# GraphSAGE neighbour sums on one core: the source one-hots are made in their load buffers, 36 buckets in each of five

## The chip, the core and the metric

The kernel runs on one core of a Trainium2 chip. The metric is the device time of one execution in microseconds, start to end. The core's engines each work through their own queue in order: TensorE (PE, with its weight loads shown apart as PEld), VectorE (DVE), ScalarE (ACT), GpSimd (POOL) and SyncE (SP, which here only starts transfers). Transfers between device memory and the on-chip memory are carried by DMA engines. An engine that needs the result of another waits on semaphores.

## What is computed

There are 12,500 nodes with 64 features each, and 800,000 edges with a random source and a random destination. Each node gets the sum of the features of its neighbours, scaled by `deg_inv`, multiplied by one 64 x 64 matrix, and its own features multiplied by another:

```python
N, deg, D = 12500, 64, 64
E = N * deg
src = randint(0, N, E); dst = randint(0, N, E)
nsum = segment_sum(x[src], dst, N)          # one row for each destination
h_neigh = nsum * deg_inv[:, None]
return x @ w_self + h_neigh @ w_neigh
```

## The kernel before, in words

The kernel sorts the edges and then turns the gather and the scatter into matrix products with one-hot matrices. Nodes are cut into 98 source blocks of 128 nodes (`NB`) and 77 destination blocks of 164 nodes, each of two halves of 82 (`HN`). A pair of a destination block and a source block is a **bucket**: there are 77 x 98 = 7546 of them (`NBID`), and each holds at most 64 edges to either half in 128 slots; the few that do not fit are **leftovers**. The first 800 us sort the edges on DVE (sorting steps and merges, lines 260, 316, 328, 362) and write, for each bucket, the source number of each slot to a table `sl` in device memory, and the destination number of each slot to `dlT` on the chip.

The part that the change touches is `nodes`. It handles the buckets in groups of 8, called **tiles** here, 943 of them. For one tile:

- PE makes 8 products `ct` (line 945): the one-hots of the sources of a bucket (`ohs`, as weights) times the features of the source block (`xh`). This picks the source rows.
- ACT (line 955), or for some late tiles DVE (line 953), copies `ct` from the accumulators to `xg`.
- PE makes 16 products into `acc` (line 1025): `xg` (as weights) times the one-hots of the destinations (`ohd`). This adds the rows up by destination.

The one-hots come in chunks of 28 buckets from `one_hots`. For each chunk, SP loads the source numbers, repeated over all 128 partitions, into `slb` with four transfers (line 912, three buffers); DVE compares them with the partition number and writes `ohs` (line 914, three buffers of its own); DVE compares the destination numbers in `dlT` with a ramp and writes `ohd` (line 919, four buffers). `AHEAD` says how many buckets must have their one-hots written, in program order, beyond the tile that PE is given: 44, so that a chunk is asked for at the first tile where fewer than 52 are ready.

Nothing but the order in which the program is written sets the order of work on an engine. Into the DVE queue go, between the one-hots, pieces of the merges that still have to be done for the later parts of the sort. They are given out by `PACE`: 330 ns of merge work (by the program's own estimate) for each tile while one part is merged, 265 ns while the next is. When the first merges of a part are through, `split_rows` stores the rows, counts them, and has POOL gather them in eight transfers (line 556); the merges after that (first line 316) read what was gathered. Its last `yield` says how many tiles pass before those merges are put in the queue.

Leftovers are added by `pick` (POOL fetches their source rows into `lx`, line 976), `spread` (DVE makes their destination one-hots `ohl`, line 985) and `add` (PE, line 993). `HELD` is the number of `lx` and `ohl` buffers, five. POOL also issues the gathers of the sort and adds the finished rows to the output (line 1101).

## Time and profile before

| what | value |
|---|---|
| median of three runs | 1874.64 us (1874.48 to 1878.96) |
| time of the profiled execution | 1869.61 us |
| its span, first to last instruction | 1867.8 us |
| mean granted TensorE clock | 0.806 |
| first load of source numbers (start of `nodes`) | 802.7 us |
| start of the last one-hot of sources on DVE | 1845.3 us |
| ACT copies `xg`, line 955 | 918, 862.4 us busy |
| DVE copies `xg`, line 953 | 32, 39.0 us busy |
| DVE source one-hots, line 914 | 270, 323.6 us busy |
| DVE destination one-hots, line 919 | 270, 362.0 us busy |

Times are counted from the first instruction of the span. In a row of a wait, the engine and line that waited stand first, then what released it, then the microseconds in total, how often, and the longest. In rows of a group of instructions stand the busy time, the mean in ns of one, and the idle time before them with what ended it. In the rows of a timeline stand the start, the duration, the engine, the line and the operation, and in brackets the idle time before it and its releaser.

### The profile page before, as it was taken

How to read it: one execution, taken by the hardware profiler on the slowest of the kernel's cores; microseconds unless marked ns; L12 is line 12 of the kernel's file. 1: busy time of each engine (PE TensorE's matmuls, PEld its weight loads, DVE VectorE, ACT ScalarE, POOL GpSimd, SP SyncE). 2: the span in 40 equal slices, each digit the busy share in tenths (PEclk: the TensorE clock that was granted, in tenths of full speed). 3: DMA queues.
4: the chain of work that ended last, by engine and by line, in shares of the span. 5: the costliest groups of instructions: out<-in, count | busy, mean ns of one | idle time of the engine just before them, and what ended most of it. 6: DMA issues, size and time to landing. Idle time of an engine off the chain costs nothing.

```text
span 1867.8 us, 54105 instructions
## 1 busy us (share of the span) xinstructions
PE 974.5 (52%) x23374; PEld 844.1 (45%) x23374; DVE 1730.9 (93%) x1731; ACT 1126.5 (60%) x1592; POOL 565.5 (30%) x447
## 2 busy tenths in 40 slices
PE   0035100000000000058878989897888999889996
PEld 0014100000000000057767878776777888778885
DVE  8999999999999999989979999999986999888985
ACT  7263100113001005457989999899898999878885
POOL 2000000055512005404535445473315324431331
PEclk9997555555555555579999999999999999989998
DMA  4306200021002002168968898987897899978994
GB/s 156 71 0 161 45 0 0 37 78 51 17 5 71 11 0 81 48 205 248 283 207 261 268 269 255 288 264 221 221 307 204 286 272 269 300 190 269 278 266 128
DMA packets 176788, 307.77 MB, mean 165 GB/s; under 512 B 127885, under 2 KB 133340, under 8 KB 175772
## 3 DMA queue, kind: packets, MB, share of 16 engines
q1 hardware_dynamic: 98268, 275.58, 45.3%
q0 software_dynamic: 78272, 28.65, 9.4%
q8 instruction: 184, 3.01, 0.6%
q14 instruction: 64, 0.52, 0.1%
HBM read 277.01 MB, written 26.52 MB: 163 GB/s over the span
## 4 chain that ended last, share of the span: by engine, by line
DVE 20%; PE 15%; issue 10%; DMA 9%; ACT 7%; SPq 4%; POOL 2%; DVEq 0%; ACTq 0%; POOLq 0%
DMA slb<-sl 8%; PE ct L945 8%; DVE u L328 7%; PE acc L1025 6%; ACT xg L955 5%; SPq L912 4%; DVE ohs L914 4%; DVE ohd L919 3%; DVE u L362 2%; DVE u L316 1%; POOL out L1101 1%; PE acc L993 1%; PE po L1092 1%; POOL u L556 0%; DMA lx<-xt,ls 0%
## 5 line engine op out<-in xcount | busy, mean ns | idle before, releaser
L955 ACT ACTIVATE xg<-ct 128x1024 f16<-128x1024 f32 x918 | 862.4, 1059 | 115.1 <-PE ct L945 71.9
L945 PE MATMUL ct<-xh,ohs 128*128 128x128 f16 x7546 | 529.6, 222 | 76.9 <-DVE ohs L914 24.3
L945 PEld LDWEIGHTS <-ohs 128*128 128x128 f16 x7546 | 447.2, 99 | 116.3 <-DVE ohs L914 54.8
L328 DVE TENSOR_TENSOR u<-u 128x1512 f32<-128x1512 f32 (+57 forms) x316 | 427.0, 1362 | 12.0 <-ACT u L312 7.9
L1025 PE MATMUL acc<-ohd,xg 64*128 64x82 f16 x15092 | 401.2, 201 | 56.3 <-issue 29.4
L1025 PEld LDWEIGHTS <-xg 64*128 64x128 f16 x15092 | 326.4, 96 | 117.0 <-issue 42.5
L914 DVE TENSOR_SCALAR ohs<-slb,pidx 128x3584 f16<-128x3584 bf16 x270 | 323.6, 1198 | 48.5 <-PE ct L945 22.6
L976 POOL DMA_INDIRECT lx<-xt,ls x127 | 227.4, 1791 | 460.9 <-PE acc L993 386.0
L919 DVE TENSOR_TENSOR ohd<-iota,dlT 128x2296 f16<-128x2296 bf16 x270 | 362.0, 1341 | 0.0
L500 PE MATMUL stp<-cx,swapa 128*128 128x16 f32 (+1 forms) x12 | 3.1, 335 | 394.3 <-DVE swapa L496 394.3
L260 DVE TENSOR_TENSOR a<-b 128x1040 f32<-128x1040 f32 (+41 forms) x130 | 194.7, 1539 | 4.0 <-DVE b L260 0.5
L260 DVE TENSOR_TENSOR b<-a 128x1040 f32<-128x1040 f32 (+46 forms) x150 | 194.6, 1345 | 3.2 <-ACT a L262 0.4
L529 POOL DMA_INDIRECT u<-d,ixa x48 | 72.5, 1510 | 391.4 <-ACT junka L517 335.7
L500 PEld LDWEIGHTS stp<-cx,swapa 128*128 128x128 f32 x12 | 2.6, 272 | 394.9 <-DVE swapa L496 210.3
L312 ACT ACTIVATE u<-u 128x256 f32<-128x256 f32 (+14 forms) x60 | 32.9, 611 | 163.5 <-DVE u L316 127.6
L1101 POOL DMA_DIRECT2D out<-o x27 | 100.9, 3866 | 94.1 <-ACT o L1095 75.8
L791 PE MATMUL tr<-idb,l 128*128 128x128 bf16 x59 | 7.8, 269 | 189.0 <-ACT l L785 189.0
L262 ACT ACTIVATE b<-a 128x2 f32<-128x2 f32 (+31 forms) x41 | 15.9, 401 | 130.0 <-DVE a L260 119.7
L791 PEld LDWEIGHTS <-l 128*128 128x128 bf16 x59 | 4.4, 116 | 191.3 <-ACT l L785 190.9
L316 DVE TENSOR_TENSOR u<-u 128x2016 f32<-128x2016 f32 (+11 forms) x40 | 62.5, 1574 | 18.0 <-DMA lx<-xt,ls 16.0
L262 ACT ACTIVATE a<-b 128x1 f32<-128x1 f32 (+24 forms) x34 | 8.6, 258 | 111.0 <-DVE b L260 105.6
L953 DVE CAST xg<-ct 128x1024 f16<-128x1024 f32 x32 | 39.0, 1221 | 22.5 <-PE ct L945 19.3
(157 smaller groups left out, 825.3 us busy)
## 6 DMA issues: line engine op xcount, KB each, us to landing
slb<-sl SPq DMA_DIRECT2D x1076, 224.0 KB
xt<-xh SPq DMA_DIRECT2D x1, 3136.0 KB
out<-o POOLq DMA_DIRECT2D x25, 123.0 KB
own<-os SPq DMA_DIRECT2D x12, 256.0 KB
out<-os SPq DMA_DIRECT2D x12, 256.0 KB
rd<-dst SPq DMA_DIRECT2D x4, 521.0 KB
rs<-src SPq DMA_DIRECT2D x4, 521.0 KB
lx<-xt,ls POOLq DMA_INDIRECT x127
```

Of the source, the lines that this page charges most:

```text
L260: nc.vector.tensor_tensor(view(dst, lo + sh, [[st, g], [1, l]]), x, y, op=op)
L316: nc.vector.tensor_tensor(at(oth, to, n), x, y, op=op)
L328: nc.vector.tensor_tensor(to, at(cur, ln + lo, n), at(cur, lo + k, n), op=op)
L529: nc.gpsimd.indirect_dma_start(out=u[:, i * w:(i + 1) * w], out_offset=None, in_=src, in_offset=bass.IndirectOffsetOnAxis(ap=self.start[pa ...
L912: nc.sync.dma_start(b[j::4], bass.AP(tensor=src.tensor, offset=src.offset, ap=[[0, 32], [1, n * 128]]))
L914: nc.vector.tensor_scalar(s.rearrange("p c s -> p (c s)"), b, self.pidx[:, :1], None, op0=OP.is_equal)
L919: nc.vector.tensor_tensor(d, self.iota[:, None].to_broadcast(wide), ix, op=OP.is_equal)
L945: nc.tensor.matmul(ct[:, i * 128:(i + 1) * 128], cols[i][0], self.xh[:, (b0 + i) % NB].rearrange("p a f -> p (a f)"), start=True, stop=True)
L955: nc.scalar.activation(xg[:, :cnt * 128], ct[:, :cnt * 128], AF.Copy)
L976: nc.gpsimd.indirect_dma_start(out=x, out_offset=None, in_=self.xt, in_offset=bass.IndirectOffsetOnAxis(ap=self.left[p][1][:, c:c + 1].bit ...
L1025: nc.tensor.matmul(acc[h][:, db % OCT * HN:(db % OCT + 1) * HN], xg[r, i * 128:(i + 1) * 128], d[r], start=db % OCT == 0 and sb == 0, stop ...
L1101: nc.gpsimd.dma_start(out, o[:n, at], accum_op=OP.add)
```

## The change

Every edit is in the supply of one-hots or near it:

- The loads write straight into the buffers `ohs`, and DVE writes the source one-hots over the numbers it compares, in place (both types are 16 bits wide). There are five such buffers of 36 buckets in place of three of `slb` and three of `ohs` of 28. So there are 210 source chunks for 270, and a load of 1,179,648 bytes for 917,504.
- The destination one-hots keep 28 buckets to a chunk and get a fifth buffer. The two kinds are now asked for apart: destinations at 60 buckets ahead, sources at 76 (`AHEAD` plus `FURTHER`).
- The one-hots of leftovers are stored in two blocks of 82 for each half in place of six; the comparisons are of the same size as before.
- `pick` counts a leftover buffer as taken until six tiles after its products were issued (`BACK`), so POOL is not sent for a row while its buffer is still read.
- `split_rows` lets nine tiles pass in place of five before the next merges are queued.
- `fill(4e3)` puts some 4 us of merges into the DVE queue ahead of the first one-hots.

```diff
@@ -63,7 +63,7 @@
 BIGBITS = 0x7E000000
 BIG = float(np.array(BIGBITS, np.uint32).view(np.float32))
 SIG = 5.5
-AHEAD = 44
+AHEAD = 60
 APART = 30
...
 SIGMA = 6.0
@@ -71,7 +71,11 @@
 BEHIND = 5e3
 NEARLY = 24
 LAG = 4
+FURTHER = 16
+SCH = 36
+DCH = 28
 HELD = 5
+BACK = 6
 OCT = 6
 OCTM = 256 // OCT + 1
 assert all((b * OCTM) >> 8 == b // OCT for b in range(NDB))
@@ -558,7 +562,7 @@
                 in_offset=bass.IndirectOffsetOnAxis(ap=ix[:, j:j + 1], axis=0))
             self.pause(1)
             yield 1
-        yield 5
+        yield 9
 
     def merge_runs(self, lens, u, pong, nruns, last=False):
 
@@ -900,34 +904,43 @@
         self.left[part] = (place, s)
         yield 1
 
-    def one_hots(self, pool):
-
-
-        nc = self.nc
-        for c in range(0, NBID, 28):
-            n = min(28, NBID - c)
-            b = pool.tile([128, 28 * 128], BF, name="slb", bufs=3)[:, :n * 128]
+    def source_hots(self, pool):
+
+
+        nc = self.nc
+        for c in range(0, NBID, SCH):
+            n = min(SCH, NBID - c)
+            b = pool.tile([128, SCH * 128], BF, name="ohs", bufs=5)[:, :n * 128]
             src = self.sl[c:c + n]
             for j in range(4):
                 nc.sync.dma_start(b[j::4], bass.AP(tensor=src.tensor, offset=src.offset, ap=[[0, 32], [1, n * 128]]))
-            s = pool.tile([128, 28, 128], FH, name="ohs", bufs=3)[:, :n]
-            nc.vector.tensor_scalar(s.rearrange("p c s -> p (c s)"), b, self.pidx[:, :1], None, op0=OP.is_equal)
-            d = pool.tile([128, 14, HN, 2], FH, name="ohd", bufs=4)[:, :n // 2]
+            s = b.bitcast(FH)
+            nc.vector.tensor_scalar(s, b, self.pidx[:, :1], None, op0=OP.is_equal)
+            yield [s[:, j * 128:(j + 1) * 128] for j in range(n)]
+
+    def dest_hots(self, pool):
+
+
+        nc = self.nc
+        for c in range(0, NBID, DCH):
+            n = min(DCH, NBID - c)
+            d = pool.tile([128, DCH // 2, HN, 2], FH, name="ohd", bufs=5)[:, :n // 2]
             at = c % TURN
             wide = [128, n // 2, HN, 2]
             ix = self.dlT[:, at:at + n].rearrange("p (c t) -> p c t", t=2)[:, :, None, :].to_broadcast(wide)
             nc.vector.tensor_tensor(d, self.iota[:, None].to_broadcast(wide), ix, op=OP.is_equal)
-            yield [(s[:, j], d[:, j // 2, :, j % 2]) for j in range(n)]
+            yield [d[:, j // 2, :, j % 2] for j in range(n)]
 
     def nodes(self, pool, aps, mps):
 
 
         nc = self.nc
-        source = self.one_hots(pool)
-        ready = []
+        sources, dests = self.source_hots(pool), self.dest_hots(pool)
+        ready, spare = [], []
         pend = []
         late = []
         done = []
+        added = []
         acc = None
 
         turn = 0
@@ -937,15 +950,20 @@
             nonlocal turn
             ct = aps.tile([128, 1024], F32, name="ct", bufs=3)
             ahead = AHEAD - 8 * vector
-            while len(ready) < min(cnt + ahead, NBID - b0):
-                ready.extend(next(source))
-            cols = ready[:cnt]
+            rest = NBID - b0
+            while len(ready) < min(cnt + ahead + FURTHER, rest) or len(spare) < min(cnt + ahead, rest):
+                if len(ready) <= len(spare) + FURTHER and len(ready) < rest:
+                    ready.extend(next(sources))
+                else:
+                    spare.extend(next(dests))
+            cols = list(zip(ready[:cnt], spare[:cnt]))
             del ready[:cnt]
+            del spare[:cnt]
             for i in reversed(range(cnt)):
                 nc.tensor.matmul(ct[:, i * 128:(i + 1) * 128], cols[i][0],
                                  self.xh[:, (b0 + i) % NB].rearrange("p a f -> p (a f)"), start=True, stop=True)
             xg = pool.tile([128, 1024], FH, name="xg", bufs=6)
-            if vector and (len(ready) < min(8 + ahead, NBID - b0 - cnt) or NBID - b0 < 56):
+            if vector and (len(spare) < min(8 + ahead, NBID - b0 - cnt) or NBID - b0 < 56):
                 turn += 1
             else:
                 vector = False
@@ -966,7 +984,8 @@
                         uses.append([o, p, c, f // NB, -(-e // NB), None, None, None])
 
         def pick(b0):
-            if self.picked == len(done) or len([u for u in uses if u[5]]) >= HELD:
+            held = len([u for u in uses if u[5]]) + len([n for n in added if n > len(done) - BACK])
+            if self.picked == len(done) or held >= HELD:
                 return
             u = next((u for u in uses if not u[5]), None)
             if u and u[1] in self.left and b0 + LEAD >= u[4] * NB:
@@ -980,17 +999,19 @@
 
         def spread(u):
             o, p, c, f, e = u[:5]
-            u[7] = pool.tile([128, 2, OCT * HN], FH, name="ohl", bufs=HELD)
+            assert e - f <= 2
+            u[7] = pool.tile([128, 2, 2 * HN], FH, name="ohl", bufs=HELD)
             n = slice((f - o * OCT) * HN, (e - o * OCT) * HN)
-            nc.vector.tensor_scalar(u[7][:, :, n], self.wide.rearrange("p (h n) -> p h n", h=2)[:, :, n],
+            nc.vector.tensor_scalar(u[7][:, :, :(e - f) * HN], self.wide.rearrange("p (h n) -> p h n", h=2)[:, :, n],
                                     self.left[p][0][:, c:c + 1], -float(o * (OCT * HN + 4096)),
                                     op0=OP.subtract, op1=OP.is_equal)
 
         def add(u, stop=False):
             o, _, _, f, e = u[:5]
+            added.append(len(done))
             n = slice((f - o * OCT) * HN, (e - o * OCT) * HN)
             for h in range(2):
-                nc.tensor.matmul(acc[h][:, n], u[5], u[7][:, h, n], start=False, stop=stop)
+                nc.tensor.matmul(acc[h][:, n], u[5], u[7][:, h, :(e - f) * HN], start=False, stop=stop)
 
         def extras(b0, cnt):
             o = b0 // (OCT * NB)
@@ -1284,6 +1305,7 @@
             t += 1400 if i < 4 else 2800
             if k < KPRS[0]:
                 t = fill(t) if t > 0 else t
+        fill(4e3)
         va.close()
         first_two.close()
 
```

The first place where the order moves is the queue of SP in the steady part of `nodes`. In the rows, `DMAHW` are the semaphores of earlier transfers, `DVE_49` and `PE_49` those of the engines. Before, two chunks of loads and the start of a third:

```order
L912 DMA slb<-sl 32x3584 [waits DMAHW5_49,DVE_49]
L912 DMA slb<-sl 32x3584 [waits DMAHW6_49]
L912 DMA slb<-sl 32x3584 [waits DMAHW7_49]
L912 DMA slb<-sl 32x3584 [waits DMAHW0_49]
L912 DMA slb<-sl 32x3584 [waits DMAHW1_49,DVE_49]
```

The same place of the changed kernel:

```order
L916 DMA ohs<-sl 32x4608 [waits DMAHW5_49,DVE_49,PE_49]
L916 DMA ohs<-sl 32x4608 [waits DMAHW6_49]
L916 DMA ohs<-sl 32x4608 [waits DMAHW7_49]
L916 DMA ohs<-sl 32x4608 [waits DMAHW0_49]
L916 DMA ohs<-sl 32x4608 [waits DMAHW1_49,DVE_49,PE_49]
```

The first of the four transfers of a chunk waited for DVE alone, which had read the buffer; now it waits for PE as well, which has to be through with the one-hots that stand in it.

The second place is the queue of DVE where the gathered rows of the second part are first read (the merge of 4 x 368, line 316 before and 320 now). Before, with the waits of each instruction (`DMASW` are POOL's transfers, here the gathers):

```order
L914 TENSOR_SCALAR ohs_4924<-slb_4919,pidx_88 128x3584 [waits DMAHW3_49,DMAHW2_49,DMAHW4_49,DMAHW1_49,PE_49]
L919 TENSOR_TENSOR ohd_4926<-iota_109,dlT_1165 128x2296 [waits PE_49]
L985 TENSOR_SCALAR ohl_4970<-wide_111,lp0_2318 128x2x164
L328 TENSOR_TENSOR u_790<-u_786 128x8x102 [waits DVE_49]
L914 TENSOR_SCALAR ohs_5048<-slb_5043,pidx_88 128x3584 [waits DMAHW6_49,DMAHW5_49,DMAHW7_49,DMAHW0_49,PE_49]
L919 TENSOR_TENSOR ohd_5050<-iota_109,dlT_1165 128x2296
L316 TENSOR_TENSOR u_782<-u_778 128x4x368 [waits DMASW4_49,DMASW3_49,DMASW6_49,DMASW2_49,DMASW7_49,DMASW1_49,DMASW0_49]
```

The same place of the changed kernel (ohs is line 918 there, ohd 931, ohl 1005):

```order
L918 TENSOR_SCALAR ohs_4468<-ohs_4468,pidx_88 128x4608 [waits DMAHW6_49,DMAHW7_49,DMAHW5_49,DMAHW0_49]
L931 TENSOR_TENSOR ohd_4485<-iota_109,dlT_1165 128x2296 [waits PE_49]
L1005 TENSOR_SCALAR ohl_4529<-wide_111,lp0_2309 128x328
L332 TENSOR_TENSOR u_790<-u_786 128x8x102 [waits DVE_49]
L1005 TENSOR_SCALAR ohl_4588<-wide_111,lp0_2309 128x2x82
L918 TENSOR_SCALAR ohs_4591<-ohs_4591,pidx_88 128x4608 [waits DMAHW3_49,DMAHW4_49,DMAHW2_49,DMAHW1_49]
L931 TENSOR_TENSOR ohd_4597<-iota_109,dlT_1165 128x2296 [waits PE_49]
L332 TENSOR_TENSOR u_790<-u_786 128x8x101
L320 TENSOR_TENSOR u_782<-u_778 128x4x368 [waits DMASW5_49,DMASW3_49,DMASW6_49,DMASW2_49,DMASW1_49]
```

A source one-hot waited for its four loads and for PE, which had to leave its buffer; now it waits for the loads alone. A destination one-hot now waits for PE at nearly every chunk. Source and destination chunks no longer come in pairs.

The third place is the start of `nodes` on DVE, before (line 846 is the last work of the sort's first part there):

```order
L846 MAX top0_1472<-e_1471 128x8 x5
L914 TENSOR_SCALAR ohs_1667<-slb_1662,pidx_88 128x3584
L919 TENSOR_TENSOR ohd_1669<-iota_109,dlT_1165 128x2296
L914 TENSOR_SCALAR ohs_1676<-slb_1671,pidx_88 128x3584
L919 TENSOR_TENSOR ohd_1678<-iota_109,dlT_1165 128x2296
L316 TENSOR_TENSOR u_778<-u_782 128x1264
```

And in the changed kernel:

```order
L850 MAX top0_1472<-e_1471 128x8 x5
L320 TENSOR_TENSOR u_778<-u_782 128x1264
L332 TENSOR_TENSOR u_782<-u_778 128x219 x2
L332 TENSOR_TENSOR u_778<-u_782 128x969 x2
L918 TENSOR_SCALAR ohs_1670<-ohs_1670,pidx_88 128x4608
L931 TENSOR_TENSOR ohd_1676<-iota_109,dlT_1165 128x2296
L918 TENSOR_SCALAR ohs_1678<-ohs_1678,pidx_88 128x4608
L931 TENSOR_TENSOR ohd_1684<-iota_109,dlT_1165 128x2296
L918 TENSOR_SCALAR ohs_1686<-ohs_1686,pidx_88 128x4608
L931 TENSOR_TENSOR ohd_1692<-iota_109,dlT_1165 128x2296
L332 TENSOR_TENSOR u_782<-u_778 128x1173
```

The merge that stood behind two chunks of each kind, and the smaller ones behind it, now stand ahead of the first source one-hot, and three chunks of each kind follow.

## The prediction

> **What bounds the kernel now.** I cut the time from the first load of source numbers into stretches, and read in each what the engines do.
>
> ```profile
> span 1867.8 us, 54105 instructions
> ```
>
> ```profile
> core 0: us, PE busy (x) PEld busy (x) DVE busy (x) ACT busy (x) POOL busy (x), PEclk, DMA share, GB/s
> 802.70:860.00 57.30, 39.26 (x852) 34.47 (x853) 50.48 (x84) 36.26 (x41) 11.30 (x10) 0.81 0.78 248
> 860.00:950.00 90.00, 78.87 (x1947) 68.78 (x1944) 72.44 (x76) 80.52 (x109) 47.36 (x35) 0.94 0.86 256
> 950.00:1200.00 250.00, 221.55 (x5768) 194.68 (x5764) 247.87 (x242) 234.20 (x279) 108.68 (x43) 1.00 0.87 262
> 1200.00:1600.00 400.00, 350.17 (x8712) 305.24 (x8711) 367.57 (x478) 368.71 (x492) 167.47 (x107) 0.97 0.86 259
> 1600.00:1850.00 250.00, 224.43 (x5789) 200.68 (x5789) 218.88 (x269) 209.05 (x261) 74.89 (x49) 0.97 0.83 250
> ```
>
> Before 802.7 us nothing but the order of a few instructions is touched. In 950 to 1200 DVE has no idle time (247.87 of 250) while ACT has 15.8 and PE 28.4: here DVE sets the pace. After 1200 DVE has slack (32.4 and 31.1), and ACT and PE alternate as the bound. So I asked for the waits of 950 to 1200 (from 940, to take in a stall ahead of it), then for those of the whole run:
>
> ```profile
> PE ct L945 <- DVE ohs L914: 20.4, 24, 3.0
> ACT xg L955 <- PE ct L945: 17.4, 24, 2.4
> DVE u L316 <- DMA lx<-xt,ls: 9.3, 1, 9.3
> ```
>
> ```profile
> PE ct L945 <- DVE ohs L914: 24.3, 31, 3.0
> DVE ohs L914 <- PE ct L945: 22.6, 14, 5.7
> DVE ohs L914 <- DMA slb<-sl: 15.3, 8, 5.6
> POOL lx L976 <- PE acc L993: 386.0, 78, 15.1
> ```
>
> Of the 24.3 us in which PE stands for a source one-hot, 20.4 fall here, and ACT stands with it (17.4). Those 20.4 us are what the change can win back; the other 3.9 are scattered. DVE's own waits for PE (22.6) show the other side: with three `ohs` buffers DVE may not run ahead. The stall is this one, on DVE's and PE's timelines:
>
> ```profile
> 931.93 0.99 DVE L328 TENSOR_TENSOR u<-u 128x816 f32<-128x816 f32 x1
> 937.67 2.01 DVE L914 TENSOR_SCALAR ohs<-slb,pidx 128x3584 f16<-128x3584 bf16 x1 [4.74 <-remote]
> 939.61 1.33 DVE L919 TENSOR_TENSOR ohd<-iota,dlT 128x2296 f16<-128x2296 bf16 x1
> 950.21 1.69 DVE L316 TENSOR_TENSOR u<-u 128x1472 f32<-128x1472 f32 x1 [9.26 <-DMA lx<-xt,ls]
> 951.82 1.15 DVE L914 TENSOR_SCALAR ohs<-slb,pidx 128x3584 f16<-128x3584 bf16 x1
> ```
>
> ```profile
> 953.02 1.07 PE L945 MATMUL ct<-xh,ohs 128*128 128x128 f16 x16 [2.97 <-DVE ohs L914]
> 956.95 0.62 PE L945 MATMUL ct<-xh,ohs 128*128 128x128 f16 x8 [1.58 <-DVE ohs L914]
> ```
>
> DVE stands 9.26 us for the gathered rows (the releaser is named `lx`; line 316 reads what line 556 gathers), no source one-hot is finished from 939.7 to 953.0, and PE runs dry for 2.97 and 1.58 us. DVE enters its busiest stretch with no lead.
>
> **The change part by part.** Products per stretch give the time of a bucket:
>
> ```profile
> 950.00:1200.00 250.00, 130.41 (x1892) 108.50 (x1892) 1.00 0.87 262
> 1600.00:1850.00 250.00, 130.46 (x1902) 112.64 (x1902) 0.97 0.83 250
> ```
>
> 250 / 1892 = 0.132 us a bucket, 1.06 us a tile of 8.
>
> *Fewer, longer one-hots.* In a quiet place one follows another like this:
>
> ```profile
> 1005.93 1.14 DVE L914 TENSOR_SCALAR ohs<-slb,pidx 128x3584 f16<-128x3584 bf16 x1
> 1006.99 1.34 DVE L919 TENSOR_TENSOR ohd<-iota,dlT 128x2296 f16<-128x2296 bf16 x1
> ```
>
> ```profile
> L914 DVE TENSOR_SCALAR ohs<-slb,pidx 128x3584 f16<-128x3584 bf16 x13 | 14.9, 1146 | 0.1
> L914 DVE TENSOR_SCALAR ohs<-slb,pidx 128x1792 f16<-128x1792 bf16 x1 | 0.7, 676 | 0.0
> ```
>
> 1.06 us pass from start to start. The two sizes (last 68 us of the run) give (1146 - 676) / 1792 = 0.262 ns an element, so 3584 elements take 0.94 us and 0.12 is fixed; 4608 take 1.06 + 0.27 = 1.33. Sixty fewer instructions save 60 x 0.12 = 7.2 us of DVE in all. In 950 to 1200 there are 1892 / 28 = 67.6 of them now and 52.6 after: 15 x 0.12 = **1.8 us** on the bound. The rest falls where DVE has slack, worth nothing but a part of the scattered 3.9 us; I take **2** for those, with the deeper buffers, bounds 0 and 3.9. The trace has no such comparison in place. Bounds: the same speed, since the bytes read and written are the same, or half the speed (+0.94 us each, 49 us in the stretch). I take the same; half is part of the last rival.
>
> *More lead.* Before, chunk c may be written only when PE has left chunk c-3, 56 buckets before PE needs it: at best 56 x 0.132 - 1.06 = 6.3 us of lead. After, the load must have landed, and DVE asks 84 to 76 buckets ahead: 84 x 0.132 - 1.33 = 9.8 us if the load is in time (below). That is **3.5 us** more to spend before PE stands; bounds 0 (loads late) and 3.5. Each such spending counts once for the stretch, since DVE cannot rebuild a lead there.
>
> *Later merges after a gather, `BACK`.* Four more tiles are 4 x 1.06 = 4.2 us, which could come off the 9.26; but in the order seven destination chunks stand between the count and the first merge as before, and two leftover fetches now stand among the eight gathers on POOL. Bounds 0 and 9.3; I take **3.3**. POOL's 386 us of waiting were off the path; only a gather behind it was on it.
>
> *4 us of merges moved ahead.* DVE has an idle place for them:
>
> ```profile
> 808.19 1.15 DVE L914 TENSOR_SCALAR ohs<-slb,pidx 128x3584 f16<-128x3584 bf16 x1 [5.62 <-DMA slb<-sl]
> 811.49 1.15 DVE L914 TENSOR_SCALAR ohs<-slb,pidx 128x3584 f16<-128x3584 bf16 x1 [0.88 <-DMA slb<-sl]
> ```
>
> They fit in the 5.62 us while the first load runs (without it they would cost 4). At 330 ns a tile the merging then ends 12 tiles sooner. The waits left beside the two gaps are 20.4 - 4.6 = 15.8 us over 236 tiles, 0.067 each: **0.8 us**.
>
> *Start.* The two loads landed 3.30 us apart, 917,504 bytes: 278 GB/s. The first load grows by 262,144 bytes, 0.94 us, and its one-hot by 0.27: **1.2 us lost**. The order asks for three chunks of each kind before any merge, so DVE idles between them as it did.
>
> *The new wait.* SP now waits for PE before it loads a chunk. Nothing else is queued on SP in this part. The buffer of chunk c is free 144 buckets before PE needs it, and DVE asks 84 to 76 before: 60 to 68 buckets, 7.9 to 9.0 us, for four issues and the landing. In the chain of waits, a usual load and a slow one:
>
> ```profile
> 1026.62 0.45 SPq L912
> 1028.53 4.20 DMA slb<-sl
> 1091.40 0.45 SPq L912
> 1093.94 6.50 DMA slb<-sl
> ```
>
> From the first issue to the landing: 6.1 and 9.0 us. With 0.94 us for the bytes, or everything 36/28 as long, 7.0 to 7.9 and 10.0 to 11.6. The usual load just makes it, the slow one is 1 to 3.7 us late for DVE, but still 7 us early for PE (144 x 0.132 = 19.0). I charge nothing. The Trainium skill ("DMA: Bandwidth & Descriptors", anatomy of one DMA) gives about 2.0 us plus bytes over 436 GB/s for a transfer, measured on POOL's path: as an estimate 4.1 us for the old chunk, with which the 4.20 row agrees, and 4.7 for the new one. By it a load grows by 0.6 us and not 0.94, and the sum would be better by 0.3.
>
> ```profile
> 1009.40 4.17 POOL L1101 DMA_DIRECT2D out<-o  x1 [0.20 <-issue]
> 1009.95 2.36 DVE L914 TENSOR_SCALAR ohs<-slb,pidx 128x3584 f16<-128x3584 bf16 x1
> ```
>
> ```profile
> L914 DVE TENSOR_SCALAR ohs<-slb,pidx 128x3584 f16<-128x3584 bf16 x269 | 322.9, 1200 | 48.5 <-PE ct L945 22.6 <-DMA slb<-sl 15.3 <-remote 4.7
> ```
>
> A one-hot beside a transfer that POOL issues takes twice as long; over all it is 1200 - 1146 = 54 ns each. If that went with their number, 15 fewer would save another 0.8 us. The Trainium skill ("SBUF — State Buffer", two separate sides) has DVE and POOL hold a shared port pair in turn, the loser blocked: then stretches go with POOL's instructions, which stay. I leave the 0.8 out.
>
> **Sum**, against the profiled execution: 1.8 + 2 + 3.5 + 3.3 + 0.8 - 1.2 = **10.2 us** less, 1869.6 to 1859.4 (span 1857.6). The median shown is 5.0 us above that execution, so 1874.6 to **1864.4 us**.
>
> **Rivals.**
>
> *The stalls go altogether.* If lead, less work and the shorter stall add up so that DVE never falls behind, all 24.3 us go: 1874.6 - 24.3 + 1.2 = 1851.5. For it: 3.5 + 3.3 + 1.8 already is near half of 20.4, and the one-hots for the destinations get 16 buckets more too. Against it: DVE stays without idle time.
>
> *Work, not lead.* If DVE's work alone sets 950 to 1200 and the gather stays where it is, only 1.8 and the start remain: 1874.6 - 1.8 + 1.2 = 1874.0, no change. For it: 247.87 of 250.
>
> *The loads enter DVE's queue.* A late load stops DVE in front of a source one-hot, and with it destination one-hots, merges and the late copies behind it. If every fourth load is slow when DVE is on time, 13 in 950 to 1200, each about 2.35 us late, DVE loses 31 us. It has 2.1 us of idle time there, so 29 come on top: 1864.4 + 29 = 1893, slower than before. In 1600 to 1850 the same loss would fit into its 31.1 us. It decides from 10.2 / 2.35, five such loads, on. Against it: a DVE that is behind finds its load landed, so the waits come only when there is lead to lose.
>
> **How the numbers follow.** Forecast 0.45, stalls gone 0.20, no change 0.20, loads in the way 0.15 (a slower comparison in place is in it). A change under 0.3% (5.6 us) cannot be told from none here. Faster 0.65, same 0.20, slower 0.15. The forecast's own range is 1857 to 1869; for 8 times in 10 I take 1847 to 1881, which holds the first three and cuts the last.
>
> **What would show it.** Right: PE's waits for source one-hots in that stretch fall from 20.4 to about 10 us and ACT's for PE with them; DVE has few waits for loads; 210 source one-hots at about 1.33 us from start to start; the stretch that does 236 tiles shortens by 8 to 10 us. Wrong: waits of DVE for loads above 40 us; one-hots in place much over 1.4 us; the 9.26 us stall unchanged with PE still dry behind it.

## The result, and the profile after the change

The changed kernel took **1902.92 us** (median of four runs, 1894.99 to 1913.25) against 1876.8 us of the kernel before in the same rounds (1874.48 to 1879.4): a ratio of 1.0149, 95% interval 1.0118 to 1.0181. I had forecast 1864.4 us, in a range up to 1881. It became slower by some 28 us, and the range does not hold it. The profiled execution took 1903.88 us.

First the page of the changed kernel (span, the source one-hots, and the instruction queue):

```profile
span 1902.1 us, 54017 instructions
L918 DVE TENSOR_SCALAR ohs<-ohs,pidx 128x4608 f16<-128x4608 bf16 x210 | 306.7, 1460 | 59.6 <-DMA ohs<-sl 58.7
q8 instruction: 186, 3.05, 0.6%
```

and one of these comparisons in a quiet place, with the instruction behind it:

```profile
954.51 1.41 DVE L918 TENSOR_SCALAR ohs<-ohs,pidx 128x4608 f16<-128x4608 bf16 x1
955.84 1.34 DVE L931 TENSOR_TENSOR ohd<-iota,dlT 128x2296 f16<-128x2296 bf16 x1
```

In place the comparison is as fast as it was: 1.33 us from start to start, as forecast, 1460 ns on average for 4608 elements where 3584 took 1198, and all of them together cost 306.7 us in place of 323.6. So the work did get less. The stretches with the same bounds as before (columns as in the prediction):

```profile
860.00:950.00 90.00, 76.49 (x1768) 66.55 (x1766) 68.68 (x71) 74.69 (x103) 53.13 (x35) 0.90 0.76 244
950.00:1200.00 250.00, 224.69 (x5738) 198.84 (x5730) 244.37 (x229) 232.13 (x280) 116.09 (x42) 0.97 0.79 263
1200.00:1600.00 400.00, 341.71 (x8407) 298.03 (x8403) 347.43 (x433) 356.68 (x473) 163.92 (x103) 0.96 0.75 246
1600.00:1850.00 250.00, 217.62 (x5507) 193.47 (x5505) 206.82 (x251) 203.06 (x258) 86.12 (x54) 0.97 0.77 252
```

The count behind PE's time tells how far the work got. In 950 to 1200, where I had looked for the gain, PE did 5738 matmuls in place of 5768: nothing was won. In 1200 to 1600 it did 8407 in place of 8712, in 1600 to 1850 5507 in place of 5789. At 23 matmuls a microsecond (5738 / 250) these 587 are 26 us. The 179 that are missing in 860 to 950 would be another 8, and together this is the 34 us by which the span is longer; but the kernel with the edits beside the one-hots alone (below) is behind at 950 as well, with 1815 matmuls in that stretch, and isn't slower in the end. What engines wait for, over the whole run, after the change:

```profile
PE acc L1046 <- issue: 45.4, 64, 2.6
PE ct L963 <- issue: 32.1, 45, 2.4
PE ct L963 <- DVE ohs L918: 22.4, 1, 22.4
DVE ohs L918 <- DMA ohs<-sl: 58.7, 36, 5.7
DVE u L320 <- DMA u<-da,ixb: 12.4, 2, 10.9
SPq L916 <- PE ct L963: 401.5, 161, 8.1
```

and the two rows of before that answer to the first two:

```profile
PE acc L1025 <- issue: 29.4, 55, 2.2
PE ct L945 <- issue: 10.8, 24, 1.5
```

PE stands for source one-hots once, at the start (22.4 us; before, that wait had the load's name and took 21.4). The 24.3 us of before are gone. Two other waits grew in their place. DVE stands 58.7 us for loads, 15.3 before. And PE stands 77.5 us where the profile names nothing that it waits for, 40.2 before. The first kind on DVE's timeline, the second on PE's:

```profile
1353.13 1.34 DVE L931 TENSOR_TENSOR ohd<-iota,dlT 128x2296 f16<-128x2296 bf16 x1
1355.86 1.42 DVE L918 TENSOR_SCALAR ohs<-ohs,pidx 128x4608 f16<-128x4608 bf16 x1 [1.39 <-DMA ohs<-sl]
```

```profile
1350.65 0.45 PE L1046 MATMUL acc<-ohd,xg 64*128 64x82 f16 x13
1353.67 0.51 PE L1046 MATMUL acc<-ohd,xg 64*128 64x82 f16 x17 [2.57 <-issue]
```

The second stall lies in the midst of the products of one tile, and the profile shows nothing that PE waits for there. The packets of queue q8 explain it. There are 186 of 16,384 bytes in the run; one began to move at 1351.45 us, took 0.95 us, and PE went on 1.27 us after it had landed. Counting over the trace, 64 of PE's unnamed stalls (57.9 us) end 1.2 to 1.6 us after such a packet has landed, and 58 of them lie at the same place, within two, in blocks of 256 PE instructions; 16,384 bytes are 64 for each instruction of a block. So PE runs out of instructions and fetches the next block through the same 16 DMA engines that carry the loads. Before, the same count gave 28 stalls and 18.5 us. The unnamed stalls that no such packet accounts for stayed as they were, some 22 us before and 20 after: the growth is all in late fetches. From the moment when PE starts the first instruction of a block to the start of the packet passed 2.19 us before and 2.61 us after (medians over some 175 fetches each). That is a small step, but a block lasts 5.6 us (median), of which 0.95 and 1.27 are the packet and what follows it. So, as an estimate from these figures, a fetch that starts more than some 3.3 us after its block stalls PE: 17 of 178 did before, and 53 of 181 after.

### The profile page after: what moved, and what is told of

It reads as the page before. It is cut to its first block, busy times and chain, and to the rows that moved or that the text cites. A ratio compares the mean times of both kernels' runs of the same rounds, so it can differ in the third digit from the quotient of the medians.

```text
span 1902.1 us, 54017 instructions
## 1 busy us (share of the span) xinstructions
PE 990.6 (52%) x23374; PEld 859.6 (45%) x23374; DVE 1721.3 (90%) x1673; ACT 1127.2 (59%) x1590; POOL 589.2 (31%) x447
## 2 busy tenths in 40 slices
DMA packets 165266, 307.76 MB, mean 162 GB/s; under 512 B 124045, under 2 KB 129500, under 8 KB 137500
## 4 chain that ended last, share of the span: by engine, by line
PE 34%; DVE 13%; issue 9%; ACT 7%; DMA 2%; POOL 1%; SPq 1%; another core or an unknown queue 0%; DVEq 0%; ACTq 0%; POOLq 0%
PE ct L963 18%; PE acc L1046 14%; DVE u L332 5%; ACT xg L973 4%; DMA ohs<-sl 2%; DVE u L366 2%; DVE ohs L918 1%; DVE ohd L931 1%; PE acc L1014 1%; PE po L1113 1%; SPq L916 1%; DVE u L320 1%; DMA sl<-l 1%; ACT u L316 1%; ACT g L1053 0%
## 5 line engine op out<-in xcount | busy, mean ns | idle before, releaser
L963 PE MATMUL ct<-xh,ohs 128*128 128x128 f16 x7546 | 540.6, 225 | 76.0 <-issue 32.1
L963 PEld LDWEIGHTS <-ohs 128*128 128x128 f16 x7546 | 457.4, 101 | 113.6 <-issue 66.9
L332 DVE TENSOR_TENSOR u<-u 128x1512 f32<-128x1512 f32 (+56 forms) x316 | 427.5, 1364 | 16.8 <-ACT u L316 13.0
L995 POOL DMA_INDIRECT lx<-xt,ls x127 | 252.5, 1988 | 425.8 <-PE acc L1014 338.3
L918 DVE TENSOR_SCALAR ohs<-ohs,pidx 128x4608 f16<-128x4608 bf16 x210 | 306.7, 1460 | 59.6 <-DMA ohs<-sl 58.7
L971 DVE CAST xg<-ct 128x1024 f16<-128x1024 f32 (+1 forms) x33 | 39.8, 1207 | 38.5 <-PE ct L963 34.4
```

Source lines behind the costliest of these rows:

```text
L332: nc.vector.tensor_tensor(to, at(cur, ln + lo, n), at(cur, lo + k, n), op=op)
L918: nc.vector.tensor_scalar(s, b, self.pidx[:, :1], None, op0=OP.is_equal)
L963: nc.tensor.matmul(ct[:, i * 128:(i + 1) * 128], cols[i][0], self.xh[:, (b0 + i) % NB].rearrange("p a f -> p (a f)"), start=True, stop=True)
L995: nc.gpsimd.indirect_dma_start(out=x, out_offset=None, in_=self.xt, in_offset=bass.IndirectOffsetOnAxis(ap=self.left[p][1][:, c:c + 1].bit ...
```

## The experiments

All were timed beside the kernel before; the ratios come from several executions, the rows of waits from one each. Names in capitals are theories. In the first four SIZE puts the loss down to the size of a chunk's load, DEPTH to the number of buffers, LOCK to one-hots that are written where they were loaded; the later ones are explained in the expectation that first has them. A last table puts all runs side by side.

**Size or place.** The change with 28 buckets in six buffers, as large as before but in place:

```diff
-SCH = 36
+SCH = 28
-            b = pool.tile([128, SCH * 128], BF, name="ohs", bufs=5)[:, :n * 128]
+            b = pool.tile([128, SCH * 128], BF, name="ohs", bufs=6)[:, :n * 128]
```

> The changed kernel, but with 28 buckets in each of six in-place buffers (load rows of 7168 bytes as before the change, 168 buckets in all instead of 180). Theory SIZE (the fetches of PE's instructions wait in the DMA rings behind the rows of the loads, and a row of 9216 bytes holds them longer): PE's idle time put down to issue falls from 77 us toward the 40 of before, and the time to about 1865. Theory LOCK (PE itself releases the loads, so they come in step with its own fetches, whatever their size): issue stays near 77 us and the time near 1900. Theory DEPTH (more loads stand in the rings at once): with six buffers no better than 1900.

Measured: 1862.13 us, **0.9963** of before (0.9936 to 0.9989), with these waits:

```profile
PE acc L1046 <- issue: 27.6, 26, 2.5
PE ct L963 <- issue: 19.4, 17, 2.6
DVE ohs L918 <- DMA ohs<-sl: 41.5, 32, 3.0
```

So writing in place, the two generators, the extra lead and the moved merges are together not what costs. The 36 buckets are, or their five buffers in place of six; the last experiment takes these two apart.

**Rows in two pieces.** Each load's rows were to be cut in two:

```diff
-                nc.sync.dma_start(b[j::4], bass.AP(tensor=src.tensor, offset=src.offset, ap=[[0, 32], [1, n * 128]]))
+                half = n * 64
+                nc.sync.dma_start(b[j::4].rearrange("p (a s) -> p a s", a=2),
+                                  bass.AP(tensor=src.tensor, offset=src.offset, ap=[[0, 32], [half, 2], [1, half]]))
```

> The changed kernel, but each row of a load written as two pieces of 4608 bytes, with the same four transfers, buffers and order. SIZE: if the rings take the pieces one by one, issue falls to 40 us or less, time about 1860. LOCK and DEPTH: unchanged, 77 us and about 1900. If the two pieces are joined again by whoever makes the descriptors, nothing changes under any theory; the count of DMA packets tells (some 6700 more per 100 chunks if they are not).

Measured: 1887.86 us, 1.011 (1.0071 to 1.0149). The pieces touch each other and went as one packet all the same, as the count shows, which is that of the change to the last one (before the change: 176,788):

```profile
DMA packets 165266, 307.76 MB, mean 163 GB/s; under 512 B 124045, under 2 KB 129500, under 8 KB 137500
```

It decides nothing on rows, and repeats the change: issue waits of 62.0 us, waits for loads of 65.1.

**The edits beside.** The kernel before with the moved merges (`fill(4e3)`, `yield 9`), `BACK` and narrow leftover one-hots, and nothing of the source one-hots:

```diff
-        yield 5
+        yield 9
...
+        fill(4e3)
```

> The kernel before, with the edits beside the buffers alone: 4 us of merges ahead of the first one-hots, nine tiles for five after a gather, leftover buffers counted as taken for six tiles more, narrow leftover one-hots. If the loss sits in the in-place buffers, as all three theories have it: PE's issue stays at 40 us, and the time is 1866 to 1874 (a part of the 3.3 + 0.8 us of the forecast). If the loss sits in these edits: about 1900.

Measured: 1870.72 us, 1.0013 (0.9978 to 1.0048): no difference.

**Four buffers.** The change with `bufs=4`.

> The changed kernel with four in-place buffers of 36 instead of five. DEPTH: fewer loads stand in the rings at once, issue falls well under 77 us; time under 1890 unless the source one-hots now come late. SIZE and LOCK: issue stays near 77 us; the loads are released 36 buckets (4.8 us) later, DVE waits for them much more than 59 us, PE stands for source one-hots again, and the time is 1910 to 1960.

Measured: 1935.5 us, 1.0375 (1.0311 to 1.0439). The waits for loads double, PE's issue waits do not grow:

```profile
PE acc L1046 <- issue: 31.1, 33, 2.4
PE ct L963 <- issue: 11.6, 13, 2.0
DVE ohs L918 <- DMA ohs<-sl: 117.2, 59, 7.7
```

With a buffer less a load is asked for later, and DVE pays: the time lies where SIZE and LOCK had it. But of the issue waits DEPTH was right: they fell to 42.7 us, though a fetch is as late as in the change (2.62 us in the median, 55 of 181 later than 3.3). So a late fetch seems to cost less in a kernel that loses its time elsewhere, and the two rows aren't prices that can be added.

**Short rows.** The load cut by columns: four transfers of 128 partitions with a quarter of the columns each, for the change, and for 28 buckets in six buffers.

```diff
+            m = n * 32
             for j in range(4):
-                nc.sync.dma_start(b[j::4], bass.AP(tensor=src.tensor, offset=src.offset, ap=[[0, 32], [1, n * 128]]))
+                nc.sync.dma_start(b[:, j * m:(j + 1) * m], bass.AP(tensor=src.tensor, offset=src.offset + j * m, ap=[[0, 128], [1, m]]))
```

> The change (36 buckets, 5 buffers) with each chunk's load cut by columns: four transfers of all 128 partitions and a quarter of the columns in place of four transfers of 32 partitions and all columns; so rows of 2304 bytes in place of 9216, the same bytes per chunk and the same number of transfers. The change lost by waits of PE put down to issue: 77.5 us against 40.2 before, and all of its further loss of time (28 us) has to be explained from there. ROW (a fetch of PE's instructions stands behind rows of the loads that are already under way, so its delay goes with the length of a row): the issue waits fall to 25 us or less, below those of before, and the time to 0.98 to 0.995 of before. BURST (the delay goes with the bytes of a chunk that are queued at once, 1.18 MB against 0.92): nothing changes, issue waits 65 to 85 us, time 1.010 to 1.018 of before. LOCK (not the loads but one-hots written where they were loaded): as BURST, 1.010 to 1.018.

> One-hots in place, 28 buckets in six buffers, and each chunk's load cut by columns into quarters: rows of 1792 bytes in place of 7168. With whole rows this kernel had issue waits of 47.0 us and 0.9963 of the time before. ROW: issue waits below 25 us, time 0.98 to 0.99 of before. BURST: issue waits 40 to 55 us, 0.993 to 0.999. LOCK: the same as BURST.

Measured: 1903.51 us, 1.015 (1.0106 to 1.0193), and 1890.12 us, 1.0093 (1.0055 to 1.0131). ROW falls: rows a quarter as long left the issue waits at 74.0 us, and with 28 buckets they rose from 47.0 to 69.9, which no theory had (BURST and LOCK: 40 to 55):

```profile
PE acc L1047 <- issue: 42.3, 65, 1.8
PE ct L964 <- issue: 27.6, 34, 2.1
DVE ohs L919 <- DMA ohs<-sl: 51.8, 40, 8.1
```

This pair (28 buckets with whole rows, 28 with quarters) is the plainest in the study: buffers, bytes, one-hots and order are the same, only the form of the transfers differs, and 1.3% goes. With 36 buckets the same edit changed nothing (1.0150 for 1.0149). A transfer in the new form takes SyncE 0.475 us from start to start in place of 0.636 (medians over the trace), so the same bytes are asked for faster. That gave the next theory, PACE.

**Small chunks.** The change with 20 buckets in nine buffers, two transfers of 64 partitions a chunk.

> The change with 20 buckets in each of nine buffers and two transfers of 64 partitions per chunk: rows of 5120 bytes, 0.66 MB a chunk, as much buffer memory as the change, and 378 one-hot operations in place of 210. ROW and BURST: both sizes fall by 0.56, so issue waits of 15 to 35 us (before: 40.2 with 7168 bytes and 0.92 MB); VectorE's one-hots cost 168 instructions more, some 10 to 15 us spread over 1000 us in which VectorE isn't always last; time 0.985 to 1.000 of before. LOCK: issue waits of 65 us or more and a time of 1.010 or more.

Measured: 1877.41 us, 1.0003 (0.9982 to 1.0024); DVE waits 11.5 us for loads, but PE's issue waits are 55.9 us, above the 15 to 35 that BURST gave for a chunk of this size, and the time isn't below that of before. So a small chunk alone isn't enough. With two transfers in place of four, 320 KB go out with each issue.

**Half of the loads.** The kernel before, with 14 of each 28 buckets loaded and read twice; this leaves out half of the source loads, and with them the right one-hots of the other half.

```diff
-            src = self.sl[c:c + n]
+            src = self.sl[c:c + n // 2]
...
-            nc.vector.tensor_scalar(s.rearrange("p c s -> p (c s)"), b, self.pidx[:, :1], None, op0=OP.is_equal)
+            nc.vector.tensor_scalar(s.rearrange("p (t c) s -> p t (c s)", t=2), b[:, None, :].to_broadcast([128, 2, m]),
+                                    self.pidx[:, :1], None, op0=OP.is_equal)
```

> The kernel before, but a chunk of 28 buckets loads only 14 of them (rows of 3584 bytes, half of the bytes), and its one-hot operation reads the loaded half twice: this leaves out half of the source loads and makes the second half of each chunk's one-hots from the wrong sources; all other work, and the number of instructions, is as before. It prices the loads by themselves. ROW and BURST: issue waits of PE fall from 40.2 us to 20 or less; the waits for one-hots stay at 20 to 30 us, if they are not for the loads; time 0.98 to 0.992 of before. LOCK: the loads are not what delays the fetches; issue waits stay at 33 to 45 us and the time at 0.996 to 1.002 of before.

Measured: 1851.85 us, 0.9856 (0.9818 to 0.9894), against 1877.08.

```profile
PE acc L1027 <- issue: 12.2, 25, 1.6
PE ct L947 <- issue: 5.8, 18, 0.7
DVE ohs L915 <- DMA slb<-sl: 6.3, 4, 4.8
```

The loads are what delays the fetches: from block start to packet start 0.93 us in place of 2.19, and the issue waits fall from 40.2 to 18.0 us. LOCK falls. It also says what the loads cost the kernel *before* the change: 25 us for half of them, more than the 15.3 us that stand in a row with their name.

**Pace.** Four kernels that change only the bytes per issue of SyncE: before with two transfers of 64 partitions, before with seven of four buckets, the change with six of twelve buckets by 64 partitions, 28 buckets in place with seven. The last form, for instance:

```diff
-            for j in range(4):
-                nc.sync.dma_start(b[j::4], bass.AP(tensor=src.tensor, offset=src.offset, ap=[[0, 32], [1, n * 128]]))
+            for j in range(0, n, 4):
+                w = min(4, n - j) * 128
+                nc.sync.dma_start(b[:, j * 128:j * 128 + w], bass.AP(tensor=src.tensor, offset=src.offset + j * 128, ap=[[0, 128], [1, w]]))
```

> The kernel before, with each chunk of 28 buckets loaded by two transfers of 64 partitions in place of four of 32: the same rows, the same bytes, the same buffers, but 448 KB per issue of SyncE in place of 224 KB. An issue takes SyncE 0.59 us either way, so what is asked for per us of issuing doubles. PACE (the fetches of PE's instructions stand behind whatever source loads are issued and not yet landed; that backlog was 590 KB on average before, 661 KB in the change, 180 KB with half of the loads, and it grows with the bytes that SyncE hands out per us): backlog above 680 KB, PE's issue waits from 28 to 40 us to 50 to 80 us, time 1.004 to 1.015 of before. FREED (the backlog grew because the buffers come free late, from PE, and not because of the size of an issue): backlog and issue waits as before, time 0.998 to 1.003.

> The kernel before, with each chunk of 28 buckets loaded by seven transfers of all 128 partitions and four buckets: 128 KB per issue, which in this form takes SyncE 0.43 us (start to start 0.475), so 270 KB per us in place of 352. PACE: backlog below 520 KB, issue waits below 25 us, time 0.985 to 0.996 of before. FREED: as before, 0.997 to 1.003, or slower by the seven issues.

> The change (36 buckets in each of five buffers) with each chunk loaded by six transfers of 64 partitions and twelve buckets: 192 KB per issue of 0.59 us, 302 KB per us in place of 453. PACE: backlog 520 to 600 KB in place of 661, issue waits 25 to 45 us in place of 77.5, time 0.990 to 1.004 of before in place of 1.015. FREED: issue waits 60 to 80 us, time 1.010 to 1.018.

> One-hots in place, 28 buckets in six buffers, each chunk loaded by seven transfers of 128 partitions and four buckets, 270 KB per us of issuing (with four transfers of 32 partitions, 352 KB per us, this kernel had 0.9963 of the time before; with four of 128 partitions, 472 KB per us, 1.0093). PACE: backlog below 560 KB, issue waits below 30 us, time 0.985 to 0.995. FREED: issue waits 45 to 70 us and a time of 0.996 to 1.010, without regard to the size of an issue.

Measured: 1.0021 (1.0000 to 1.0043), 1.0723 (1.0679 to 1.0767), 1.0136 (1.0096 to 1.0177) and 1.0744 (1.0701 to 1.0786). The first and the third time lie where FREED had them. The two slow ones lie far above every figure given (FREED had allowed for the first of them "slower by the seven issues"). Before with seven transfers:

```profile
PE acc L1026 <- issue: 9.5, 18, 1.7
PE ct L946 <- issue: 5.8, 11, 1.9
DVE ohs L915 <- DMA slb<-sl: 172.0, 112, 7.6
SPq L913 <- DMA slb<-sl: 71.9, 142, 2.0
```

The backlog and the issue waits came down as PACE said, to 452 thousand bytes and 15.3 us, but SyncE now stands for its own earlier transfers and the loads come late: DVE loses 172 us, and the time rises by 134. The change with six transfers:

```profile
PE acc L1048 <- issue: 32.2, 58, 2.7
PE ct L965 <- issue: 15.0, 29, 1.6
DVE ohs L920 <- DMA ohs<-sl: 76.6, 59, 3.6
```

Here the backlog fell as PACE said (565 thousand bytes), 30 us of issue waits went, 18 us of waits for loads came, and the time stayed. So slower asking trades the one cost for the other. And doubling the bytes per issue of the kernel before raised the mean backlog (to 675 thousand bytes from 590) and neither the issue waits (38.6 us) nor the time much: PACE alone doesn't hold either.

**When DVE asks.** The loads as in the change, only DVE's asking is moved: `FURTHER` 0, then also `AHEAD` 44, for 36 buckets in five buffers and for 28 in six.

```diff
-AHEAD = 60
+AHEAD = 44
-FURTHER = 16
+FURTHER = 0
```

> The change with FURTHER 0 in place of 16: VectorE asks for a chunk of source one-hots when 60 to 68 buckets are left in place of 76 to 84, so a load has 16 buckets (2.1 us) more between the release of its buffer by PE and the moment when VectorE stands for it; loads, buffers and all else as in the change. LATE (the change lost because VectorE, with little idle time, stands behind loads that are not there yet: 58.7 us against 15.3 before): VectorE's waits for loads below 30 us, time 0.990 to 1.002 of before. FETCH (it lost because the fetches of PE's instructions stand behind the loads; the waits of VectorE cost little): issue waits of PE stay at 60 to 80 us and the time at 1.008 to 1.018.

> The change with FURTHER 0 and AHEAD 44 (both as before the change, where source and destination one-hots were asked for together, 44 to 52 buckets ahead): 32 buckets (4.2 us) more for a load than in the change. LATE: VectorE's waits for loads below 12 us, PE's waits for source one-hots back at 5 to 20 us, time 0.988 to 1.000 of before. FETCH: issue waits of PE 60 to 80 us, time 1.008 to 1.018.

> One-hots in place, 28 buckets in six buffers (0.9963 of before, VectorE's waits for loads 41.5 us, PE's issue waits 47.0), now with FURTHER 0. LATE: VectorE's waits for loads below 20 us, time 0.984 to 0.993 of before. FETCH: time 0.994 to 1.000, with issue waits of 40 to 55 us.

> The same with AHEAD 44 as well: 32 buckets more for each load than with FURTHER 16 and AHEAD 60. LATE: VectorE's waits for loads below 10 us; PE's waits for source one-hots 5 to 20 us; time 0.984 to 0.996 of before. FETCH: 0.994 to 1.002.

Measured, in this order: 1.0105 (1.0062 to 1.0147), 1.0102 (1.0056 to 1.0148), 0.9977 (0.995 to 1.0004), 0.9967 (0.994 to 0.9995). DVE's waits and PE's, 36 buckets with both numbers as before:

```profile
PE ct L963 <- DVE ohs L918: 45.0, 11, 22.5
PE acc L1046 <- issue: 44.4, 43, 2.8
PE ct L963 <- issue: 28.5, 27, 2.6
DVE ohs L918 <- DMA ohs<-sl: 23.4, 8, 5.4
```

and 28 buckets:

```profile
PE acc L1046 <- issue: 24.2, 27, 2.9
PE ct L963 <- issue: 21.5, 19, 2.8
DVE ohs L918 <- DMA ohs<-sl: 13.6, 8, 3.1
```

With 36 buckets 35 of the 43 us by which DVE's waits for loads had grown are gone, and of the 1.49% about a third: 1.0102 against 1.0149, with intervals that overlap, so this third is likely and not shown. Nor does it price the late loads by themselves: with less lead PE's waits for source one-hots came back, 45.0 us for the 22.4 of the change (22.5 of either is the start), so what DVE saved was in part lost on PE. With 28 buckets, moving the asks changes nothing. FETCH had all four times and the issue waits, and LATE none of the times; but DVE's waits never fell as low as LATE had supposed. What is left, 1.0102 against 0.9967, is 25 us, and stands beside 27 us of issue waits and 10 of waits for loads.

**Size, once more.** The same order of work with 24 buckets in seven buffers and 32 in five.

> In place, FURTHER 0, AHEAD 44, 24 buckets in each of seven buffers, four transfers of 32 partitions: 192 KB per issue (302 KB per us of issuing). With 28 in six buffers (352 KB per us) this was 0.9967 of before, with 36 in five (453) 1.0102. SIZE (what costs is how much each chunk asks for at once, by PE's instruction fetches and by late loads together): issue waits 25 to 42 us (28: 45.7; 36: 72.9), VectorE's waits for loads below 14 us; 53 comparisons more than with 28 buckets, some 6 us of VectorE; time 0.990 to 0.998 of before. BUFFERS (28 buckets were better for another reason, such as six buffers in place of five or how the chunks of 28 fall together with the destination chunks of 28): time 0.999 or more.

> In place, FURTHER 0, AHEAD 44, 32 buckets in each of five buffers: 256 KB per issue, 403 KB per us, between the two sizes already run, and with fewer buckets of buffer in all (160) than either (168 and 180). SIZE: issue waits 50 to 68 us, time 1.000 to 1.008 of before. BUFFERS: as 36 in five buffers or slower, 1.009 to 1.020, since buffers are as few and smaller.

Measured: 1860.33 us, **0.9960** (0.9936 to 0.9983), and 1868.14 us, 1.0000 (0.9969 to 1.0031). The waits of 24 buckets, and of 32:

```profile
PE acc L1046 <- issue: 14.7, 18, 2.2
PE ct L963 <- issue: 11.6, 9, 2.7
DVE ohs L918 <- DMA ohs<-sl: 21.4, 20, 3.2
```

```profile
PE ct L963 <- issue: 22.5, 19, 3.0
PE acc L1046 <- issue: 20.6, 25, 2.4
DVE ohs L918 <- DMA ohs<-sl: 19.1, 15, 3.6
```

SIZE had both times; of its waits, 32 buckets have less for issue (43.1 for 50 to 68) and 24 more for loads (21.4 for under 14). BUFFERS falls: five buffers of 32, the least memory of these four, beat five of 36. With the same four transfers and the same order, 24, 28, 32 and 36 buckets give 0.9960, 0.9967, 1.0000 and 1.0102. The step from 32 to 36 is the dearest.

All runs, with the two rows of waits added up from the views shown or like them. The backlog is counted from the trace: thousands of bytes of source loads that SyncE has issued and that have not landed, the mean over 860 to 1840 us; the delay is that of a fetch, as above.

```
kernel                      issues       backlog  delay  PE issue  DVE for loads  ratio
before                      4 x 224 KB     590     2.19    40.2       15.3        1
half of the loads           4 x 112        180     0.93    18.0        6.3        0.9856
before, two transfers       2 x 448        675     2.29    38.6        6.3        1.0021
before, seven               7 x 128        452     1.69    15.3      172.0        1.0723
side edits only             4 x 224        582     2.04    27.9       21.1        1.0013
the change (36 in 5)        4 x 288        661     2.61    77.5       58.7        1.0149
  rows in two (as it)       4 x 288        687     2.61    62.0       65.1        1.0110
  36 in 4                   4 x 288        646     2.62    42.7      117.2        1.0375
  quarters                  4 x 288        714     2.37    74.0       55.3        1.0150
  six transfers             6 x 192        565     2.24    47.2       76.6        1.0136
  FURTHER 0                 4 x 288        670     2.52    62.3       30.4        1.0105
  FURTHER 0, AHEAD 44       4 x 288        684     2.68    72.9       23.4        1.0102
28 in 6                     4 x 224        603     2.18    47.0       41.5        0.9963
  quarters                  4 x 224        660     2.57    69.9       51.8        1.0093
  seven transfers           7 x 128        450     2.00    21.1      200.4        1.0744
  FURTHER 0                 4 x 224        604     2.43    45.5       25.7        0.9977
  FURTHER 0, AHEAD 44       4 x 224        593     2.31    45.7       13.6        0.9967
32 in 5, both               4 x 256        618     2.28    43.1       19.1        1.0000
24 in 7, both               4 x 192        535     2.02    26.3       21.4        0.9960
20 in 9                     2 x 320        631     2.46    55.9       11.5        1.0003
```

The rows of waits vary from one execution to the next: with the loads as before, the side edits have 27.9 us of issue waits for 40.2, and rows in two, which repeat the change, 62.0 for 77.5. So a difference of some 15 us between two of these rows says little by itself.

## Why the prediction was wrong

**The step that failed** is *The new wait*: "I charge nothing." Longer loads, which start only when PE has left the buffer and which DVE now stands for sooner, brought DVE 43 us more of waiting, 58.7 us, which is past the 40 that the prediction had set as a sign of being wrong. And that they delay another customer of the same DMA engines, the fetches of PE's instructions (+37 us of issue waits), was neither a term nor a rival: the prediction doesn't mention the issue waits of before, 40.2 us.

A second step failed with it. The prediction counted PE's 20.4 us of waiting for source one-hots in 950 to 1200 as time to be won back. The wait went, and the stretch was no faster, since other waits stood in its place.

Point by point:

- *Fewer, longer one-hots*: right, and too small. In place costs nothing extra, and DVE's time for them fell by 16.9 us (323.6 to 306.7) where 60 x 0.12 gave 7.2. It was worth no time: in 950 to 1200 DVE had 5.6 us left idle, and the matmuls of that stretch fell from 5768 to 5738.
- *More lead* and the scattered waits: the mechanism was right, and went further than the forecast. Of PE's 20.4 us in that stretch nothing is left, where I had expected about 10. In their place PE has 14.7 us of issue waits there (2.8 before), and ACT still stands 14.1 us for PE (14.3 before in these bounds), where the prediction had this fall too.
- *Later merges after a gather*: not as forecast. I took 3.3 us off the stall; it is 10.9 us long, 1.6 longer than the 9.3 of before:

```profile
944.23 1.69 DVE L320 TENSOR_TENSOR u<-u 128x1472 f32<-128x1472 f32 x1 [10.89 <-DMA u<-da,ixb]
```

  It ends 6 us sooner (944.2 in place of 950.2), and the 4.74 us that DVE stood just ahead of it before, at 937.67, are gone: the two together went from 14.0 to 10.9. So DVE's idle time here did fall by 3.1 us, near the term, but by the rows landing sooner and not by a shorter wait for them; why they landed sooner isn't shown.
- *Merges moved ahead*: without the rest these edits made no difference that can be measured (1.0013, 0.9978 to 1.0048), so neither the 0.8 us nor the 3.3 shows.
- *Start*: 1.2 us forecast, 1.0 measured (22.4 against 21.4).
- *The new wait*, its size: the load itself was foreseen well. From the first issue to the last landing a chunk took some 5.9 us before and 6.8 after (medians over the trace), 0.9 more for an estimate of 0.94. One in ten took over 8 us, where I had 7.9 to 9.0 us to spend. I had seen that a slow load is 1 to 3.7 us late for DVE, and charged nothing because it is still early for PE: 36 of 210 were late, at 1.6 us each, and the work behind them in DVE's queue was late with them. The row of 4.20 us, which the prediction set beside an estimate of 4.1 for a whole chunk, follows one issue, so one transfer of 229,376 bytes, and tests nothing; the measured growth of 0.9 agrees with the 0.94 from the rows and not with the 0.6 from that estimate.

Of the rivals, *the loads enter DVE's queue* (0.15, 1893 us) has the sign, the size and the row, 58.7 us; but not the place. In 950 to 1200 it is one wait of 5.4 us for the 31 that I had worked out: the reason against it that I gave (a DVE that is behind finds its load landed) fits what happened there. In 1200 to 1600, for which I had worked out nothing and where DVE had 32.4 us of slack, it is this much, and after it PE's issue waits:

```profile
DVE ohs L918 <- DMA ohs<-sl: 36.5, 22, 5.7
PE acc L1046 <- issue: 20.5, 25, 2.6
PE ct L963 <- issue: 9.7, 14, 2.0
```

Whether it is the larger or the smaller part of the loss isn't settled by the moved asks. *The stalls go altogether* was right on PE's waits for source one-hots and wrong on the time (1851.5). *Work, not lead* had the stretch right, which did no more matmuls than before, and the time wrong (1874.0): it had no term for the loads either. Of a lead that is worth something there is one sign: 28 buckets in six buffers, with the lead of the change, did 5872 matmuls in 950 to 1200, 104 more than before, some 4.5 us.

**What stays open.** The size of a chunk's load is shown to be the cause of the loss as long as the form of the transfers and the order of the asks stay the same (24 to 36 buckets in one order). It isn't the whole rule: 28 buckets lose 1.3% by the form of the transfers alone, and 20 in nine, the smallest chunk, but with two transfers and the asks of the change, is no faster than before. How the price divides between late loads and late instructions isn't settled: their rows grow together in most kernels. The rows that hold one of them apart are the two slowest kernels (before with seven transfers: 157 us more of waits for loads, 25 less of issue waits, and a time 134 us longer), and before with two transfers, 20 in nine and 36 with later asks on the other side. Nor do I know what sets the delay of a fetch. Within the change it is longer with a backlog (1.37 us below 0.5 MB, 2.88 from there to 1.0, 2.91 above), and in kernels with four transfers of 32 partitions it goes roughly with the bytes of a row: 0.93 us for 3584 bytes, 2.02 for 6144, 2.31 for 7168, 2.28 for 8192 and 2.68 for 9216. The Trainium skill ("DMA: Bandwidth & Descriptors", queues, rings and completion order) has each DMA engine go round its queues, a whole packet of some 9 to 17 descriptors at a time. As an estimate by it, with a descriptor taken to be one row of a load, nine rows at 0.140 (3584 bytes) to 0.347 us each (9216; medians of the trace) take 1.3 to 3.1 us, which is near these five; seventeen would take twice as long. Nine of 2304 bytes, at 0.093, take 0.8, and there the delay was 2.37: with these the rule and the trace don't agree.

The clock is hardly the cause. The granted clock of PE was half for 56 us of 830 to 1850 before, and for 93 after the change; but with half of the loads it was 85 us, and that kernel is the fastest, and with 36 buckets and both numbers as before it was 59, and that one takes 1.0102.

## What to carry to other kernels

When a change makes transfers larger or later, look for everyone who uses the DMA engines, instructions too: a wait of PE named "issue" in the midst of a tile can be such a customer, and its sum over the run belongs on the list of terms. A load that lands "just in time" by medians was late here in one case of six; give it the margin of its slow tenth, and check every stretch for it, not the busiest alone. Here the gain of working in place was to be had with smaller pieces: 24 buckets in seven buffers, with the asks as before, take 0.9960 of the time before (0.9936 to 0.9983).

## What the runs showed of the hardware beyond what was expected

PE's program isn't all there when the kernel starts: 186 packets of 16 KB, 256 instructions each, come during the run, and a program of 47,200 PE instructions pays for each that is late. Two adjoining pieces of one row went as one packet (165,266 packets, as with whole rows). A transfer of 128 partitions by a quarter of the columns took SyncE 0.43 us to issue, one of 32 partitions by all columns 0.59, for the same bytes; and rows of 1024 bytes in seven transfers were slower than four transfers of 7168-byte rows, with SyncE standing 71.9 us for its own earlier transfers.
